# A fused attention and MLP block on one core: modulation, z and the last columns of w3 in column tiles and plain products, gb inside w4, a new order

## The chip, the cores and the metric

The kernel runs on one core of a Trainium2 chip. The metric is device time in microseconds (us) of one execution, the median of several runs. Five engines run their own instruction streams in order: PE multiplies matrices (PEld loads its stationary operands), DVE, ACT and POOL do elementwise work, SP issues nearly all transfers.

## The reference

S = 2048 rows, D = 512, H = 32 heads of 16, F = 1376, all in float32:

```
mod = silu(c) @ w_mod                      # 1 x 3072 = sa, ca, ga, sb, cb, gb
h   = layernorm(x) * (1 + ca) + sa
q, k, v = split(h @ wqkv)                  # 32 heads of 16
phi(t)  = concat(softmax(t @ w_phi), softmax(-(t @ w_phi)))   # 32 features a head
kv  = sum over rows of phi(k)^T v ;  z = sum over rows of phi(k)
o   = (phi(q) kv) / (phi(q) z + 1e-6)
x   = x + ga * (o @ wo)
g   = layernorm(x) * (1 + cb) + sb
s   = gelu(layernorm(g) @ w1), its four quarters shifted by +1, -1, +2, -2 rows
y   = g + s @ w2
out = x + gb * (y + gelu(layernorm(y) @ w3) @ w4)
```

## The kernel before

Rows go in eight chunks of 256, each of two tiles of 128. The attention needs kv and z over all rows before any output row, so the program has three stages: keys, values and queries of all chunks (until about 150 us), the attention's output with wo and then w1, w2 chunk by chunk (to about 370 us, beside the first half of the MLP), and the rest of the MLP (w3, gelu, w4). Most large products are made exact with fp32r halves: an operand is split into a high part and a remainder (`hi_lo`), and three products replace one (`three`). w3 and w4 are multiplied block-wise with seven products instead of eight, from sums of weight blocks and of activation blocks; the last 96 columns of w3 don't fill such a block and are treated apart (`up_last`, `load_last`, `load_w4_last`).

Names: `xl` is a tile of x, `xn` its normalized form, `pt` a transpose in PSUM (L481), `hh` the modulated and transposed chunk, `pp` general products in PSUM, `rk` raw rows of the q and k weights, which PE folds with w_phi (`bd` is w_phi as a block-diagonal matrix; one fold is 4 products of 128x128), `w` finished weights, `ke` and `qe` the features, `kva` the sum for kv, `za` the running sum of features from which z comes, `oT` the attention's output, `n` and `nT` the normalized rows of the second stage, `sh` the shifted rows, `gg` and `gl` high parts and remainders of gelu, `ac` the four accumulators of the w4 product, `uu` small temporaries, `xb` and `xc` the rows of the sum at the end. `const` is any small constant, `ones` among them.

Modulation: sa and ca are needed as columns (`mod_cols`, L532 on): the four 512 KB pieces of w_mod land as `mod2`; ca comes from products with one moving column, sa from a DVE sum and four more such products with `ones`. The other four are needed as rows that stand on all partitions (`mod_rows`, L549): 16 pieces of 256 KB are scaled by silu(c) and summed on ACT, DVE and POOL (`mod_acc`), and a product of `ones` with the sum puts the result on all partitions. z (L835) is `ones` times `za`, and eight copies take each head's piece out of it.

The order of all instructions is written out: `ORDER` is a table of operation numbers, each with a letter where it says which of DVE, ACT and POOL does it, `SLOT` one of buffer numbers. `plan.op` registers an operation with its reads and writes; `emit` issues all in the table's order, and each engine runs its share in that order. The operation's cost in `plan.op` only served to make the table. Each warm operation at the start (L501) is four products of `ones` with itself, whose result nobody reads. SP has at most eight transfers in flight.

```
def mms(items, w, r, ...):                       # products on PE; L472 issues them
def act(o, i, f, scale, bias, alts) / ts / tt / stt   # ACT; DVE or POOL where the table says so
def load(o, src, nbytes) / store(dst, i, nbytes)      # SP
```

Of the kernel before, what the change touches and what calls it, by code (L numbers as in the profile page):

```python
# [367 lines left out]
def body(ctx: ExitStack, tc, x, wqk_t, wv_d, wo_d, w1_d, w2_d, w3_d, w4_d, c_d, wmod_d, id_d, cst_d, cst2_d, out):  # L368
# [1024 lines left out]
```

## Time and profile before

| | us |
|---|---|
| median of 3 runs | 570.16 (569.96 to 570.29) |
| profiled execution | 570.87 |
| its span, first to last instruction | 569.1 |
| PE busy | 558.2 (98%) |
| DVE busy | 494.0 (87%) |
| POOL busy | 361.8 (64%) |
| ACT busy | 350.5 (62%) |
| mean granted clock of PE | 0.995 |

1.8 us of the profiled execution lie outside its span. In the rows of a timeline, the first number is when a group starts, the second how long it takes; "x" is the number of instruction records, and a product in plain float32 makes two records (two passes). What stands in square brackets is the idle time of the engine just before, and what ended it.

### The profile page before, as it was taken

Reading aid. Unit: us, or ns where it says so; the run is one execution under the profiler, and the core shown is the slowest. Engines: PE = TensorE matmul, PEld = TensorE weight load, DVE = VectorE, ACT = ScalarE, POOL = GpSimd, SP = SyncE. Lnnn points to the kernel's source line nnn. Section 1 sums busy time; section 2 is a strip of 40 time slices with the busy share of each in tenths; the row PEclk is TensorE's granted clock in tenths of the full one; section 3 lists DMA queues with packets and bytes.
Section 4 is the critical chain, followed back from the end, with each engine's and each line's share of the span. In section 5 each row is a group of like instructions: output and inputs, shape, how many; then the busy total and the mean of one; then the engine's idle time right before and its main releaser. Section 6 shows DMA issues by size and latency. Waiting matters only on the chain.

```text
span 569.1 us, 12257 instructions
## 1 busy us (share of the span) xinstructions
PE 558.2 (98%) x4460; PEld 502.4 (88%) x4460; DVE 494.0 (87%) x910; ACT 350.5 (62%) x826; POOL 361.8 (64%) x372
## 2 busy tenths in 40 slices
PE   9999999999999889999999999999999999999996
PEld 9998888788787678888879898999999999999995
DVE  3699999989899999999998777879777969898886
ACT  5699997733514767888787865865643544255530
POOL 3268978889699998998974744545444433113423
PEclk9899999999999999999999999999999999999999
DMA  8985430342646755778787896995976485828322
GB/s 327 341 270 185 168 131 29 121 131 75 222 163 238 246 157 153 288 245 313 241 263 239 299 322 226 341 357 192 390 264 219 174 285 159 324 88 272 112 75 74
DMA packets 56908, 124.06 MB, mean 218 GB/s; under 512 B 6864, under 2 KB 18384, under 8 KB 52752
## 3 DMA queue, kind: packets, MB, share of 16 engines
q1 hardware_dynamic: 56560, 123.21, 63.1%
q8 instruction: 35, 0.57, 0.4%
q14 instruction: 25, 0.20, 0.1%
q10 hardware_dynamic: 288, 0.07, 0.1%
HBM read 88.92 MB, written 34.34 MB: 217 GB/s over the span
## 4 chain that ended last, share of the span: by engine, by line
PE 83%; DVE 7%; POOL 4%; DMA 3%; ACT 1%; issue 1%; SPq 0%; DVEq 0%; POOLq 0%
PE pp L472 36%; PE pa L472 24%; PE ac L472 19%; PE pt L481 2%; DMA dram<-yt 2%; PE kva L472 1%; DVE q L443 1%; DVE pz L443 1%; POOL ez L421 1%; DMA dram<-qe 1%; POOL qe L421 1%; DMA dram<-h 1%; POOL e L421 1%; ACT n L402 1%; DVE oT L419 1%
## 5 line engine op out<-in xcount | busy, mean ns | idle before, releaser
L472 PE MATMUL pa<-bH,wq 128*128 128x256 f32 x840 | 106.8, 281 | 0.0
L472 PE MATMUL ac<-w,gg 128*128 128x256 f32 x840 | 106.0, 282 | 0.0
L472 PEld LDWEIGHTS pa<-bH,wq 128*128 128x128 f32 x840 | 103.0, 189 | 0.9 <-issue 0.2
L472 PEld LDWEIGHTS ac<-w,gg 128*128 128x128 f32 x840 | 101.8, 189 | 1.7 <-issue 1.7
L472 PE MATMUL pp<-w,hh 128*128 128x512 f32 x384 | 92.4, 396 | 0.0
L472 PEld LDWEIGHTS pp<-w,hh 128*128 128x128 f32 x384 | 71.0, 188 | 15.9
L472 PE MATMUL pp<-w,sh 128*128 128x512 f32 x192 | 49.0, 398 | 0.4 <-POOL sh L991 0.4
L472 PE MATMUL pp<-w,oT 128*128 128x512 f32 x192 | 47.6, 398 | 0.8 <-ACT oT L402 0.7
L472 PE MATMUL pp<-hh,w 128*128 128x256 f32 x384 | 48.1, 283 | 0.0
L472 PEld LDWEIGHTS pp<-hh,w 128*128 128x128 f32 x384 | 46.4, 188 | 1.9 <-issue 1.3
L472 PEld LDWEIGHTS pa<-nT,w 128*128 128x128 f32 x384 | 46.0, 188 | 1.8 <-DVE nT L419 1.0
L472 PE MATMUL pa<-nT,w 128*128 128x256 f32 x384 | 47.3, 280 | 0.1
L472 PEld LDWEIGHTS pp<-w,oT 128*128 128x128 f32 x192 | 35.4, 188 | 9.9 <-ACT oT L402 1.2
L472 PEld LDWEIGHTS pp<-w,sh 128*128 128x128 f32 x192 | 34.7, 188 | 9.3 <-issue 0.8
L582 POOL TENSOR_TENSOR rs<-mv,const 128x2 f32<-128x2 f32 x31 | 22.9, 740 | 28.3 <-ACT mv L589 28.1
L421 POOL TENSOR_TENSOR gg<-cu,gg 128x128 fp32r<-128x128 f32 (+1 forms) x25 | 17.2, 692 | 36.5 <-PE ac L472 26.7
L421 POOL TENSOR_TENSOR ez<-e,const 128x1024 f32<-128x1024 f32 x14 | 34.0, 2433 | 4.6 <-ACT const L402 4.4
L402 ACT ACTIVATE cu<-pa 128x512 f32<-128x512 f32 (+1 forms) x45 | 22.7, 516 | 19.1 <-PE pa L472 11.1
L402 ACT ACTIVATE gg<-cu 128x256 fp32r<-128x256 f32 (+1 forms) x60 | 20.2, 357 | 21.7 <-PE ac L472 11.3
L402 ACT ACTIVATE qe<-qe 128x512 f32<-128x512 f32 x32 | 19.1, 625 | 20.1 <-POOL qe L421 12.4
L419 DVE TENSOR_TENSOR gg<-sg,gg 128x512 fp32r<-128x512 f32 x37 | 26.8, 730 | 3.6 <-PE ac L472 2.5
L402 ACT ACTIVATE gg<-sg 128x512 fp32r<-128x512 f32 x37 | 22.8, 622 | 11.4 <-DVE sg L419 3.6
(215 smaller groups left out, 1299.4 us busy)
## 6 DMA issues: line engine op xcount, KB each, us to landing
wq<-dram SPq DMA_DIRECT2D x32, 1024.0 KB, 5.8
dram<-ws SPq DMA_DIRECT2D x35, 256.0 KB, 3.2
xl<-in_x SPq DMA_DIRECT2D x32, 256.0 KB, 3.7
dram<-qe SPq DMA_DIRECT2D x16, 512.0 KB, 2.9
e<-dram SPq DMA_DIRECT2D x16, 512.0 KB, 4.2
raw<-in_w SPq DMA_DIRECT2D x18, 256.0 KB, 3.8
mod<-in_wmod SPq DMA_DIRECT2D x16, 256.0 KB, 4.5
dram<-xl SPq DMA_DIRECT2D x16, 256.0 KB, 3.4
```

The source lines that it names most:

```text
L402: nc.scalar.activation(o(), i(), func, **kw)
L419: dve = ("DVE", 71 + 1.04 * o.n + 90 * (isps(a) and isps(b)), lambda: nc.vector.tensor_tensor(o(), a(), b(), op=op))
L421: pool = ("Pool", cost, lambda: nc.gpsimd.tensor_tensor(o(), a(), b(), op=op))
L443: plan.op("DVE", 65 + 1.04 * a.n + 110 * isps(o), lambda: nc.vector.tensor_reduce(o(), a(), axis=AX.X, op=op), [o], [a])
L472: nc.tensor.matmul(o(), a(), b(), start=s, stop=e, **kw)
L481: nc.tensor.transpose(o(), i(), ident())
L582: plan.op("Pool", 540 + 10 * m, lambda: nc.gpsimd.tensor_tensor(r(), v(), mhalf[:, :m](), op=OP.pow), [r], [v, mhalf])
```

## The change

Five parts and a new table.

1. **Columns.** silu(c) is copied onto 32 columns (`wide`). For each of the four `mod2` pieces, four products with 32 stationary columns and 256 moving ones stand beside each other in the four column tiles of the array, one for each half of sa and ca. ACT copies the sum, PE transposes it twice, and two DVE operations write the columns.
2. **Rows.** All four rows come from 16 products of `wide` with the 16 pieces (32 stationary, 512 moving columns, one row a column tile), accumulated in one bank. 1 is added to cb's part, four 2 KB stores put the rows into DRAM, and each row is later loaded back onto all partitions (`mod_row`). The scaling and summing on ACT, DVE and POOL goes.
3. **z.** Tiles 14 and 15 are no longer added to `za`; z is made of three parts (`za` and the two tiles) by four column-tiled products of 256 moving columns each, and one copy.
4. **The last 96 columns of w3.** `up_last` uses 96 stationary columns; in the w4 product, three products with 96 rows for each of the two tiles take the place of four with 128 and two with 64 rows.
5. **gb inside w4.** Each of the 11 pieces of w4 is multiplied by gb after it lands (four of these on DVE, seven on POOL), before the block sums are made. y * gb + x is made before the w4 product's end, so that a chunk ends with one addition and the store.
6. `ORDER` and `SLOT` are new throughout.

```diff
 ORDER = (
...
 )
...
 BIAS = {"start": 1, "late": 2, "ln_act": [1, 2, 3, 4, 5, 6, 7], "pair": [0, 1, 2, 3, 4, 5, 6, 7], "qpool": [0, 2, 4,
-        6, 8, 9, 10, 11, 12, 13, 14, 15], "tw": "any"}
+        6, 8, 9, 10, 11, 12, 13, 14, 15], "tw": "any", "zpe": [14, 15]}
...
@@ -509,49 +507,43 @@
...
-    cols = T("const", [P, 2, NK])
...
-    def mod_acc(j):
-        acc = T("acc")
-        for k in range(NK):
...
-                act(acc, raw, scale=sv[:, 0:1], alts=("DVE", "Pool"))
...
-                act(raw, raw, scale=sv[:, k:k + 1], alts=("DVE", "Pool"))
-                tt(acc, acc, raw, OP.add, "any")
-        return acc
+    cols, wide = T("const", [P, 2, NK]), T("const", [P, NK, 32])
 
     def mod_cols():
 
-        acc, p = T("acc"), T("pp", [P, 2, NK])
+        act(wide, sv[:, :, None].bc([P, NK, 32]), alts=("DVE",))
+        p, r, pc = T("pp", [P, HD]), T("mod", [P, HD]), T("pp", [P, 2, P])
         for k in range(NK):
             raw = T("mod2", [P, 2, D])
             load(raw, wmod_d[k * P:(k + 1) * P, :2 * D].rearrange("p (j n) -> p j n", j=2), 2 * P * D * 4)
-            if k == 0:
-                act(acc, raw[:, 0, :], scale=sv[:, 0:1], alts=("DVE",))
-            else:
-                stt(acc, raw[:, 0, :], sv[:, k:k + 1], acc, OP.mult, OP.add)
-            mms([(p[:, 1, b:b + 1], raw[:, 1, b * P:(b + 1) * P], sv[:, k:k + 1], k == 0 and b == 0, False)
-                 for b in range(NK)], [p], [raw, sv], skip=True)
-        mms([(p[:, 0, b:b + 1], acc[:, b * P:(b + 1) * P], ones[:, 0:1], False, b == NK - 1) for b in range(NK)],
-            [p], [acc, ones], skip=True)
+            mms([(p[32 * (2 * j + h):32 * (2 * j + h + 1)], wide[:, k, :], raw[:, j, h * HD:(h + 1) * HD], k == 0, k == NK - 1)
+                 for j in range(2) for h in range(2)], [p], [wide, raw], skip=True, tiles=4)
+        act(r, p, alts=("DVE",))
+        transp([(pc[:, i, :], r[:, i * P:(i + 1) * P]) for i in range(2)], [pc], [r])
         for j in range(2):
-            ts(cols[:, j, :], p[:, j, :], float(j), None, OP.add, None)
-
-    def mod_rows(j, plus, tag="const"):
-        acc = mod_acc(j)
-        p = T("pp")
-        mms([(p, ones, acc, True, True)], [p], [ones, acc])
+            ts(cols[:, j, :].re("p (h i) -> p h i", (2, 2), h=2).perm("p h i -> p i h", (1, 0)), pc[:, :, 64 * j:64 * (j + 1):32], float(j), None, OP.add, None)
+
+    mods = T("dram", [NK, D])
+
+    def mod_rows():
+
+        p, r = T("pp"), T("mod")
+        for k in range(NK):
+            raw = [T("mod") for _ in range(NK)]
+            for j in range(NK):
+                load(raw[j], wmod_d[k * P:(k + 1) * P, (2 + j) * D:(3 + j) * D], P * D * 4)
+            mms([(p[32 * j:32 * (j + 1)], wide[:, k, :], raw[j], k == 0, k == NK - 1) for j in range(NK)], [p], [wide, *raw],
+                skip=True, tiles=4)
+        act(r, p, alts=("DVE",))
+        ts(r[64:96], p[64:96], 1.0, None, OP.add, None)
+        for j in range(NK):
+            plan.op("SP", 475, lambda j=j: nc.sync.dma_start(mods()[j:j + 1, :], r()[32 * j:32 * j + 1, :]), [mods[:, :]], [r],
+                    lat=D * 4 / 380., land=1500 + D * 4 / 300.)
+
+    def mod_row(j, tag="const"):
         r = T(tag)
-        ts(r, p, plus, None, OP.add, None)
+        plan.op("SP", 475, lambda: nc.sync.dma_start(r(), mods()[j - 2:j - 1, :].to_broadcast([P, D])), [r], [mods],
+                lat=P * D * 4 / 380., land=2200 + P * D * 4 / 225.)
         return r
 
...
@@ -785,7 +777,7 @@
               tt_ == 0 and g < 4, tt_ == NT - 1 and g > 2 * NG - 5) for g in range(2 * NG)],
             [kva], [vv, e], skip=True, tiles=4)
         first.append(e)
-        if tt_:
+        if tt_ and tt_ not in BIAS["zpe"]:
             tt(zacc, first[0] if tt_ == 1 else zacc, e, OP.add, "any")
 
     hh0 = h_chunk(0)
@@ -809,10 +801,10 @@
             kv_add(ks[t], vs[t], c * TPC + t)
         plan.at(f"w{c}")
         if c == 1:
-            ga = mod_rows(2, 0.0, "acc")
-            cb1 = mod_rows(4, 1.0)
+            mod_rows()
+            ga = mod_row(2, "acc")
         if c == 2:
-            sb = mod_rows(3, 0.0)
+            cb1, sb = mod_row(4), mod_row(3)
...
-    zbc = T("const", [P, NG, 2 * DH])
-    for j in range(2):
-        p = T("pp", [P, NG // 2, HG, 2 * DH])
-        mms([(p.re("p g a f -> p (g a f)", (D,)), ones, zacc[:, j * D:(j + 1) * D], True, True)], [p],
-            [ones, zacc[:, j * D:(j + 1) * D]])
-        for a in range(HG):
-            act(zbc[32 * a:32 * (a + 1), NG // 2 * j:NG // 2 * (j + 1), :], p[32 * a:32 * (a + 1), :, a, :])
+    zbc, p = T("const", [P, NG, 2 * DH]), T("pp", [P, NG, 2 * DH])
+    parts = [zacc] + [e for t, e in enumerate(first) if t in BIAS["zpe"]]
+    for n, e in enumerate(parts):
+        mms([(p[32 * a:32 * (a + 1)], ones[:, :32], e.re("p (g a f) -> p g a f", (NG, HG, 2 * DH), a=HG, f=2 * DH)[:, :, a], n == 0,
+              n == len(parts) - 1) for a in range(HG)], [p], [ones, e], skip=True, tiles=4)
+    act(zbc, p)
...
     def load_last():
...
+        t = T("w", [P, 2 * NK * n9 + 2 * D], FR)
+        hi, lo = last["w3"] = [t[:, i * NK * n9:(i + 1) * NK * n9].re("p (k n) -> p k n", (NK, n9), k=NK) for i in range(2)]
+        last["w4"] = [t[:, 2 * NK * n9 + i * D:2 * NK * n9 + (i + 1) * D] for i in range(2)]
...
     def load_w4_last():
         plan.at("w42")
...
-        hi_lo(*last["w4"], raw, lo_eng="any", alts=("DVE", "Pool"))
...
+        raw, n = T("raw")[:n9], n9
+        load(raw, w4_d[2 * NP * P:, :], n * D * 4)
+        tt(raw, raw, gb[:n], OP.mult, "any")
+        hi_lo(last["w4"][0][:n], last["w4"][1][:n], raw, lo_eng="any", alts=("DVE", "Pool"))
...
@@ -1070,6 +1055,7 @@
             load(raw[i].re("p a n -> p (a n)", (D,)), w4_d[k * P:(k + 1) * P, :], P * D * 4, marks[after] if after else None)
+            tt(raw[i], raw[i], gb.re("p (a n) -> p a n", (2, HD), a=2), OP.mult, "any")
...
     plan.at("gb")
-    gb = mod_rows(5, 0.0, "gb")
+    gb = mod_row(5, "gb")
...
@@ -1190,15 +1176,11 @@
         items = []
         for k in range(NK):
             x = xs[k // 2]
-            items += three(p, last["w3"][0][:, k, :], last["w3"][1][:, k, :], x[:, 0, k % 2, :], x[:, 1, k % 2, :],
+            items += three(p[:n9], last["w3"][0][:, k, :], last["w3"][1][:, k, :], x[:, 0, k % 2, :], x[:, 1, k % 2, :],
                            k == 0, k == NK - 1)
         marks["up"] = mms(items, [p], [*last["w3"], *xs], after=marks.get("up"))
-        act(p, p, AF.Gelu_apprx_tanh)
-        act(g[:, 0, :], p)
-        for t in range(2):
-            sl = slice(t * P, (t + 1) * P)
-            tt(g[HF * t:HF * (t + 1), 1, sl], p[:HF, sl], g[:HF, 0, sl].f32(), OP.subtract)
-        tt(g[n9:, 0, :], p[n9:], g[n9:, 0, :].f32(), OP.subtract)
+        act(p[:n9], p[:n9], AF.Gelu_apprx_tanh)
+        hi_lo(g[:n9, 0, :], g[:n9, 1, :], p[:n9])
         cells[s, h, "last"] = g
...
@@ -1282,12 +1264,10 @@
             gs = ready(s, h, j)
             if j == NP - 1:
                 g = cells[s, h, "last"]
-                ps = [acc[2 + t].re("p a n -> p (a n)", (D,)) for t in range(2)]
-                sl = [slice(t * P, (t + 1) * P) for t in range(2)]
-                items = [(ps[t], g[:, 0, sl[t]], w, False, False) for t in range(2) for w in last["w4"]]
-                for t, w in enumerate((last["w4"][0], last["w4h"])):
-                    items.append((ps[t], g[HF * t:HF * (t + 1), 1, sl[t]], w[HF * t:HF * (t + 1)], False, False))
-                mms(items, acc[2:], [g, *last["w4"], last["w4h"]], skip=True, both=232)
+                for t in range(2):
+                    sl = slice(t * P, (t + 1) * P)
+                    mms(three(acc[2 + t].re("p a n -> p (a n)", (D,)), g[:n9, 0, sl], g[:n9, 1, sl], last["w4"][0][:n9],
+                              last["w4"][1][:n9], False, False), [acc[2 + t]], [g, *last["w4"]], skip=True)
...
@@ -1303,8 +1283,11 @@
         xs = []
         for t in range(TQ):
             plan.at(f"out{c * TQ + t}")
-            x1 = T("xb")
+            x1, x2 = T("xb"), T("xc")
             load(x1, x1_s[c * TQ + t], P * D * 4)
+            load(x2, x2_s[c * TQ + t], P * D * 4)
+            tt(x1, x1, gb, OP.mult, "either")
+            tt(x1, x1, x2, OP.add, "either")
             xs.append(x1.re("p (a n) -> p a n", (2, HD), a=2))
...
         for t, x1 in enumerate(xs):
-            tt_ = c * TQ + t
-            p = acc[2 + t]
+            rows_, p = slice((c * TQ + t) * P, (c * TQ + t + 1) * P), acc[2 + t]
             if c < NC - 1:
                 tt(x1, x1, p, OP.add)
-            plan.at(f"out{tt_}")
-            x1, x2 = x1.re("p a n -> p (a n)", (D,)), T("xc")
-            load(x2, x2_s[tt_], P * D * 4)
-            tt(x1, x1, gb, OP.mult, "either")
-            tt(x1, x1, x2, OP.add, "either")
-            if c < NC - 1:
-                store(out[tt_ * P:(tt_ + 1) * P, :], x1, P * D * 4)
+                store(out[rows_, :], x1.re("p a n -> p (a n)", (D,)), P * D * 4)
                 continue
-            p = p.re("p a n -> p (a n)", (D,))
             for a in range(2):
-                sl = slice(a * HD, (a + 1) * HD)
-                v = T("uu", [P, HD])
-                tt(v, p[:, sl], gb[:, sl], OP.mult)
-                tt(x1[:, sl], x1[:, sl], v, OP.add, "either")
-                store(out[tt_ * P:(tt_ + 1) * P, sl], x1[:, sl], P * HD * 4)
+                tt(x1[:, a, :], x1[:, a, :], p[:, a, :], OP.add)
+                store(out[rows_, a * HD:(a + 1) * HD], x1[:, a, :], P * HD * 4)
```

PE's start, around the columns, in the kernel before (`mod_18` and the like are the `mod2` pieces, `const_173` silu(c), `const_67` is `ones`, `const_161` the identity):

```order
L472 MATMUL pp_178<-bd_133,rk_107 128x128 x4
L472 MATMUL pp_188<-const_67 128x128 x4
L472 MATMUL pp_197<-const_67 128x128 x4
L472 MATMUL pp_210<-const_173,mod_18_109 128x1 x4
L472 MATMUL pp_210<-const_173,mod_19_111 128x1 x4
L472 MATMUL pp_210<-const_173,mod_10_89 128x1 x4
L472 MATMUL pp_210<-const_173,mod_20_113 128x1 x4
L472 MATMUL pp_210<-const_67,acc_206 128x1 x4
L472 MATMUL pp_257<-bd_133,rk_124 128x128 x4
L481 MATMUL pt_273<-const_161,xn_248 128x128
```

The same place in the changed kernel (`const_220` is `wide`, `const_110` the identity, `mod_284` the copied sum):

```order
L470 MATMUL pp_181<-bd_85,rk_69 128x128 x4
L470 MATMUL pp_195<-const_67 128x128 x4
L470 MATMUL pp_209<-const_67 128x128 x4
L470 MATMUL pp_215<-const_67 128x128 x4
L470 MATMUL pp_231<-const_67 128x128 x4
L479 MATMUL pt_244<-const_110,xn_241 128x128
...
L470 MATMUL pp_250<-mod_21_118,const_220 32x256 x4
L470 MATMUL pp_250<-mod_24_129,const_220 32x256 x4
L470 MATMUL pp_250<-mod_20_115,const_220 32x256 x4
L470 MATMUL pp_250<-mod_19_112,const_220 32x256 x4
```

Ahead of the columns stood seven warm operations, a fold and two more warm ones; now four warm operations, three folds, a warm one, a fold, four more warm ones and four transposes do. Between the columns and the first projection (`pp<-w,hh`) stood seven folds and twelve transposes; now four folds, twelve transposes and the two of the columns' sum do.

SP's stream, where the 16 w_mod pieces for the rows end in the changed kernel. They are rows 22 to 40 of the stream now; in the kernel before they were spread over rows 15 to 62:

```order
L447 DMA mod_414<-in_wmod 128x512
L447 DMA mod_452<-in_wmod 128x512
L447 DMA const_459<-in_cst 128x32
L447 DMA mod_464<-in_wmod 128x512
L447 DMA mod_502<-in_wmod 128x512
L447 DMA wr_505<-in_w 128x4x256
L447 DMA xl_518<-in_x 128x512
```

The products that read them (`pp_513`) stand on PE behind two k projections, two projections on the other operand side (`pp<-hh,w`, 24 products each) and eight transposes. The buffer of the last piece is one that held raw v weights before.

PE's end, in the kernel before (two accumulators, `ac_7568` and `ac_7549`):

```order
L472 MATMUL ac_7568<-w_2950,gl_7379 128x512 x2
L472 MATMUL ac_7549<-w_2950,gl_7379 128x512 x2
L472 MATMUL ac_7568<-w_2950,gl_7379 128x512
L472 MATMUL ac_7549<-w_4721,gl_7379 128x512
L472 MATMUL ac_7549<-w_4699,gg_7434 128x256
L472 MATMUL ac_7549<-w_4721,gg_7434 128x256
L472 MATMUL ac_7549<-w_4699,gg_7471 128x256
L472 MATMUL ac_7568<-w_4699,gg_7434 128x256
```

and in the changed one:

```order
L470 MATMUL ac_7477<-w_4723,gg_7460 128x256
L470 MATMUL ac_7472<-w_4512,gg_7302 128x256
L470 MATMUL ac_7472<-w_4636,gg_7302 128x256
L470 MATMUL ac_7472<-w_4512,gg_7338 128x256
L470 MATMUL ac_7472<-w_4646,gg_7397 128x256 x2
L470 MATMUL ac_7472<-w_4646,gg_7469 128x256
L470 MATMUL ac_7472<-w_3401,gl_7399 128x512 x3
L470 MATMUL ac_7472<-w_4723,gg_7356 128x256
```

Before, the two accumulators end nearly together; now `ac_7477` is complete twelve products ahead of `ac_7472`.

More of the change, by code (lines that the diff above doesn't have):

```diff
@@ L178 @@
-    "xn": "531f9ae64275bkai",
-    "acc": "faaf09",
-    "mod2": "1203",
-    "kva": "5",
-    "za": "1",
-    "hh": "2839cde8",
-    "pt": "54320106046160741015674650715354",
-    "raw": "k0hibd367de683l1l2e067jfi81fd",
-    "k1": "0153254515324021",
-    "ke": "4523970423790524",
-    "k2": "3011024041255323",
-    "vv": "8lh6d3b5ib2bbd2h",
-    "qe": "9701537660847318",
-    "q1": "3204341052034512",
-    "qt": "3g2hbdhfbj3f",
-    "mod": "lh37ed4gi2bj1i4e",
-    "kvs": "3",
-    "pz": "2",
@@ L225 @@
-    "uu": "g2gh4delkc92",
-    "xc": "fh716ihlfaj08jgi",
+    "pp": "220713137460513130726250130736452156623250562150350242655640233106337040236475364074236205244305"
+          "0264523076314576566475",
+    "bd": "21",
+    "w": "015647ac312085acd1472e",
+    "rk": "4305gjfc",
+    "xl": "69bh787540k8hfeld8l94dgi5kgefa9e15h3haj6h0g1g0k1",
+    "st": "14d03afdijc9e748d3jfa56a82dd5gicj",
+    "mv": "75g37c0f342fijc9e74g42f4f83h1h508",
+    "rs": "8ah6b64e718g352fiachc8gbd67ij31fd",
+    "nm": "cbei295289j1gh0a5b6dh0a1b6gh051ejb19e069b9i0372cea7246b9",
@@ new lines @@
+    "xn": "li57adhc62e1g7hf",
+    "mod": "2g02l3d6gc4ahbjif9",
+    "mod2": "2310",
+    "kva": "7",
+    "za": "3",
+    "hh": "2839bde8",
+    "pt": "62734534406134412605764776744175",
+    "raw": "ie6j3db918067i5ba3bd8b2i374k",
+    "k1": "1023412053032235",
+    "ke": "5401972654096758",
+    "k2": "4135124524302403",
+    "vv": "8kj12c23a3a427h3",
+    "qe": "7632124183485930",
+    "q1": "3205154112045012",
+    "qt": "251f2cf142if",
+    "acc": "g",
+    "kvs": "e",
+    "pz": "1",
+    "q2": "01542120",
@@ new lines @@
+    "e": "2019671475317268",
+    "ez": "9344109306823539",
+    "q3": "2342031053453415",
+    "q5": "13354132",
+    "pT": "8204364682195019",
+    "oT": "56d84596",
+    "nT": "b5edee49",
+    "n": "c3i27b7hbhci4je9",
+    "h": "6e03c42670g1f5ak",
+    "gf": "82513315",
+    "sh": "9674d74b",
+    "pa": "265074073020125713247706145423176025304315767174272605356272",
+    "wr": "88204",
+    "ws": "ai0ll7dkjc49e0h89721c8i9d9lg23k31db",
+    "gb": "l",
+    "tw": "85951",
+    "bL": "70832848",
@@ new lines @@
+    "nb": "iaj5ichae92b6a5j",
+    "yt": "c15hk4j6h0g12d4b",
+    "bH": "26413769526413251056073179124136",
+    "tr": "dc46c4ak6a697chb",
+    "wq": "9b6739e6b3096b309360b9630b3069b3069b",
+    "cu": "6cde9hbf57i24150ec3b482bge36a1c5df7a026k",
+    "gl": "ikgh7446",
+    "ac": "27366417652036057134430137645120",
+    "gg": "41097410967908794761830495637428916045287091536120305630927402598712693247051986",
+    "sg": "2i4i407gajdh7a8f7ia9icj09h59aii9be6igb19",
+    "xb": "836923dkf1j8h5kc",
+    "xc": "j28jbkjfc00k4e3d",
@@ L227 @@
+    "uu": "kikf29jg",
 }
@@ L457, in store, with mms @@
                 lat=nbytes / 380., land=1500 + nbytes / 300.)
-    def mms(items, w, r, skip=False, hold=(), after=None, duty=1.0, tiles=1, both=0):
-        cost, rec = 150 * (tiles > 1) - both, 0
+    def mms(items, w, r, skip=False, hold=(), after=None, duty=1.0, tiles=1):
+        cost, rec = 150 * (tiles > 1), 0
         for o, a, b, *_ in items:
@@ L957, in phase_a @@
         return sh, hs
-    NP, NB, n9, HF = FT // 2, 7, F - FT // 2 * 2 * P, P // 2
+    NP, NB, n9 = FT // 2, 7, F - FT // 2 * 2 * P
     w3s = T("dram", [P, NB * NP, 4 * P])
@@ L1028, in load_last @@
         plan.at("w3l")
-        t = T("w", [P, 4 * D], FR)
-        hi, lo = last["w3"] = [t[:, i * D:(i + 1) * D].re("p (k n) -> p k n", (NK, P), k=NK) for i in range(2)]
-        last["w4"] = [t[:, (2 + i) * D:(3 + i) * D] for i in range(2)]
-        raw = T("raw", [P, NK, P])
-        load(raw[:, :, :n9], w3_d[:, 2 * NP * P:].rearrange("(k p) n -> p k n", p=P), D * n9 * 4)
-        load(raw[:, :, n9:], w3_d[:, F - (P - n9):].rearrange("(k p) n -> p k n", p=P), D * (P - n9) * 4)
+        t = T("w", [P, 2 * NK * n9 + 2 * D], FR)
+        hi, lo = last["w3"] = [t[:, i * NK * n9:(i + 1) * NK * n9].re("p (k n) -> p k n", (NK, n9), k=NK) for i in range(2)]
+        last["w4"] = [t[:, 2 * NK * n9 + i * D:2 * NK * n9 + (i + 1) * D] for i in range(2)]
+        raw = T("raw", [P, NK, n9])
+        load(raw, w3_d[:, 2 * NP * P:].rearrange("(k p) n -> p k n", p=P), D * n9 * 4)
         hi_lo(hi, lo, raw, lo_eng="any", alts=("DVE", "Pool"))
@@ L1038, in load_w4_last @@
         plan.at("w42")
-        raw, n = T("raw"), F - (P - n9)
-        load(raw[:n9], w4_d[2 * NP * P:, :], n9 * D * 4)
-        load(raw[n9:], w4_d[n:, :], (P - n9) * D * 4)
-        hi_lo(*last["w4"], raw, lo_eng="any", alts=("DVE", "Pool"))
-        raw = T("raw")[HF:]
-        load(raw, w4_d[2 * NP * P:2 * NP * P + HF, :], HF * D * 4)
-        position(2 * NB * NP + 1)
-        last["w4h"] = store8[-1][:, 6:8, :].re("p a n -> p (a n)", (D,))
-        act(last["w4h"][HF:], raw, alts=("DVE", "Pool"))
+        raw, n = T("raw")[:n9], n9
+        load(raw, w4_d[2 * NP * P:, :], n * D * 4)
+        tt(raw, raw, gb[:n], OP.mult, "any")
+        hi_lo(last["w4"][0][:n], last["w4"][1][:n], raw, lo_eng="any", alts=("DVE", "Pool"))
     store8 = []
```

48 lines of the change are left out of this document (removed), and 248 rows, old and new, of the table ORDER.

## The prediction

> **What bounds the kernel now.** First the engines' busy time and the chain of work that ended last, then busy time by stretches.
>
> ```profile
> span 569.1 us, 12257 instructions
> PE 558.2 (98%) x4460; PEld 502.4 (88%) x4460; DVE 494.0 (87%) x910; ACT 350.5 (62%) x826; POOL 361.8 (64%) x372
> PE 83%; DVE 7%; POOL 4%; DMA 3%; ACT 1%; issue 1%; SPq 0%; DVEq 0%; POOLq 0%
> ```
>
> ```profile
> 0.00:10.00 10.00, 9.03 (x55) 9.03 (x56) 2.50 (x10) 4.75 (x12) 4.10 (x13) 1.00 0.82 298
> 10.00:20.00 10.00, 10.00 (x80) 10.00 (x80) 3.87 (x9) 6.26 (x14) 2.37 (x5) 0.86 1.02 375
> 200.00:250.00 50.00, 48.01 (x372) 40.46 (x371) 49.29 (x80) 40.03 (x92) 46.85 (x42) 1.00 0.62 209
> 300.00:350.00 50.00, 49.56 (x341) 45.06 (x340) 38.27 (x71) 36.06 (x99) 24.47 (x34) 1.00 0.81 283
> ```
>
> The columns of a window are its length, then busy us of PE, PEld, DVE, ACT and POOL, PE's granted clock, the transfers' share and GB/s. PE has work nearly always and carries 83% of the chain, so work that PE no longer has, or does earlier, is time won, as long as the others keep up. DVE is as full in the middle (49.29 of 50): there a gain of PE counts only if DVE loses work too. In the first 20 us PE is busy and DVE is not, and much of what PE does there is warm products that nobody reads. So the start has to be read group by group.
>
> ```profile
> 0.97 9.36 PE L472 MATMUL pp<-const 128*128 128x128 f32 x56 [0.97 <-POOL const L499]
> 12.85 3.63 PE L472 MATMUL pp<-const,mod 128*128 128x1 f32 x32
> 17.27 2.06 PE L472 MATMUL pp<-bd,rk 128*128 128x128 f32 x8
> 19.12 1.77 PE L481 MATMUL pt<-const,xn 128*128 128x128 f32 x8
> 20.73 1.95 PE L472 MATMUL pp<-bd,rk 128*128 128x128 f32 x16
> 22.51 0.60 PE L481 MATMUL pt<-const,xn 128*128 128x128 f32 x4
> 22.95 3.74 PE L472 MATMUL pp<-bd,rk 128*128 128x128 f32 x32
> 26.44 3.04 PE L472 MATMUL pp<-w,hh 128*128 128x512 f32 x12
> 29.32 1.47 PE L481 MATMUL pt<-const,xn 128*128 128x128 f32 x12
> 33.46 8.66 PE L472 MATMUL pp<-hh,w 128*128 128x256 f32 x72
> 41.96 2.97 PE L472 MATMUL pp<-w,hh 128*128 128x512 f32 x12
> ```
>
> Each row is a group: start, duration, records. One group follows right behind the other, so the difference of two starts is a group's price: the first projection's 12 products take 29.32 - 26.44 = 2.88, .24 each, and 72 of 256 moving columns 8.50, .118 each. The first projection starts at 26.44. 32 fold records take 3.49, .109 each; the 8 behind the N=1 products (one moving column) take 1.85, .23 each, and the 8 transposes then 1.61, .20 each, where four took .44. The granted clock of that window is 0.86: the N=1 products are followed by a stretch at half rate that costs 8 x .12 + 8 x .09 = 1.7 us. The first warm records are slow too: 56 in 9.36, which is about 30 at .21 and 26 at .109.
>
> **The change part by part.** *Start.* After has on PE, in this order: 32 warm records, three folds (24), a warm group (8), a fold (8), four warm groups (32), four transposes, the columns' 16 products, four transposes, two of the columns' sum, a fold, eight transposes, three folds, then the first projection. Priced by the rows above: .97 + 30 x .21 + 2 x .109 = 7.5; the next 40 records 4.4, at 11.9; four warm groups 3.5, at 15.4; four transposes .4, at 15.8. By then the columns' w_mod pieces have to be there. They and all that goes ahead of them are about 4.3 MB; at 298 GB/s up to 10 us and 375 from there they have landed by 13.5. Two normalized tiles have to be there too:
>
> ```profile
> 9.34 0.70 POOL L582 TENSOR_TENSOR rs<-mv,const 128x2 f32<-128x2 f32 x1
> 11.94 0.80 ACT L402 ACTIVATE xn<-xl,nm,rs 128x512 f32<-128x512 f32 x1
> ```
>
> x was loaded first and its scale was done at 10.04; now the weights of four folds go ahead of it, 1 MB or 2.8 us at 375 GB/s, so the scale comes at 12.9 and two normalized tiles with a small operation of .3 ahead at 14.8. Both are in time. A column tile's product is one of four that stand beside each other; the nearest row is of tiles of 64*32:
>
> ```profile
> 201.26 1.11 PE L472 MATMUL pp<-pT,const 64*32 64x256 f32 x32
> L402 ACT ACTIVATE uu<-ac 128x256 f32<-128x256 f32 x7 | 2.7, 386 | 10.5 <-PE ac L472 10.2 <-DVE xb L419 0.2
> L402 ACT ACTIVATE pt<-pt,const 128x256 f32<-128x256 f32 x20 | 10.4, 529 | 2.4 <-PE pt L481 1.5 <-DVE pt L411 0.6
> L402 ACT ACTIVATE hh<-pt 128x512 fp32r<-128x512 f32 x13 | 7.6, 594 | 0.4
> L419 DVE TENSOR_TENSOR hh<-pt,hh 128x512 fp32r<-128x512 f32 x16 | 10.7, 680 | 0.7 <-ACT hh L402 0.7
> ```
>
> 32 records of 256 columns take 1.11 us there, .035 each, where one alone takes .225 (a pass of 512 takes .45, below). So tiles do run beside each other, and I price a set of four products, two passes each, at 2 x .225 = .45: 1.8 for the columns, end at 17.6. The copy (.39) lies beside four transposes (.44); two transposes (.22) and two small DVE operations bring the columns at 18.8. PE goes on meanwhile: a fold, eight transposes and three folds, .87 + .88 + 2.6, end at 22.6. The chunk's scale, copy and remainder behind its last transpose (.53, .59, .68) end at 22.2. So the first projection starts at 23.0 (.4 for handing over) instead of 26.44, with four more transposes (.44) already done. **Gain 3.9.** If a stretch at half rate comes here too (1.7), 2.2; with nothing handed over late, 4.3.
>
> *Rows.*
>
> ```profile
> L472 PE MATMUL pp<-acc,const 128*128 128x512 f32 x8 | 4.2, 605 | 0.0
> L421 POOL TENSOR_TENSOR acc<-acc,mod 128x512 f32<-128x512 f32 x8 | 10.3, 1298 | 1.3 <-DVE acc L419 1.0
> L402 ACT ACTIVATE mod<-mod,const 128x512 f32<-128x512 f32 x10 | 7.0, 712 | 0.0
> L419 DVE TENSOR_TENSOR acc<-acc,mod 128x512 f32<-128x512 f32 x4 | 3.0, 753 | 0.1
> L438 DVE SCALAR_TENSOR_TENSOR acc<-mod,const,acc 128x512 f32<-128x512 f32 x3 | 2.3, 752 | 0.1
> L419 DVE TENSOR_TENSOR za<-za,ke 128x1024 f32<-128x1024 f32 x4 | 5.1, 1276 | 0.5 <-POOL ke L421 0.5
> ```
>
> On PE eight records, 3.6 without their overlap (.45 a pass); after, four sets of two such passes, 3.6: zero. ACT and POOL lose 7.0 and 10.3; DVE loses 3.0, the columns' 2.3 and, as the table gives it one `za` sum where it had four, 3.8: 9 us before 150 us. POOL later gets seven products of w4 with gb, 1.3 each; its 24.47 of 50 in 300 to 350 us, ahead of the first w4 product, hides them, so I count nothing; without that cover, the 9 us at POOL's 4% of the chain show .4. The stores and broadcast loads of rows: ga is needed first, for wo, whose products run around 180 us, over 100 us behind its load; nothing. The row stores stand on SP ahead of raw v weights, which are needed at about 53 us and land at about 46 by the stream's order; nothing.
>
> *z.*
>
> ```profile
> 150.04 1.88 PE L472 MATMUL pp<-za,const 128*128 128x512 f32 x4
> 151.84 0.65 PE L472 MATMUL kva<-ke,vv 128*32 128x64 f32 x32
> ```
>
> 1.80 before; three sets of two passes of .225 after, 1.35. **Gain .45.** z also no longer waits for two sums and eight copies; PE does not wait there now.
>
> *Last 96 columns.*
>
> ```profile
> 380.32 1.50 PE L472 MATMUL ac<-w,gl 128*128 128x512 f32 x6
> 381.75 1.45 PE L472 MATMUL ac<-w,gg 128*128 128x256 f32 x10
> ```
>
> 1.43 for four full products and a pair of half rows. Twelve full products of 512 columns in the chain of work:
>
> ```profile
> 72.47 2.78 PE pp L472 x12
> ```
>
> Six at that pace (.232) take 1.39, at the .24 above 1.44. Times eight, a gain of .3 to a loss of .1; I take **.2**.
>
> The Trainium skill ("TensorEngine Tiling (Array Packing)", Tiling Modes, Key Properties) says that changing the tiling mode drains TensorE. That fits the half-row pair: beside four products at .232 it leaves .50, where the pair itself is .24. By that rule the column tiles' three new stretches would cost about .27 each, and the sum would be .8 us less of a gain.
>
> *Tail.*
>
> ```profile
> 562.55 1.34 PE L472 MATMUL ac<-w,gg 128*128 128x256 f32 x9
> 565.00 0.76 DVE L419 TENSOR_TENSOR xb<-xb,uu 128x256 f32<-128x256 f32 x2
> ```
>
> PE ends at 563.89, DVE's last addition at 565.76, 1.87 later. After, one tile is added before PE ends, and two additions (.76) with .2 to start them remain. **Gain .9**; the store and the 3.3 us to the span's end stay.
>
> *Order of the middle.* PE's largest waits:
>
> ```profile
> 197.41 1.09 PE L481 MATMUL pt<-const,n 128*128 128x128 f32 x8 [1.47 <-ACT n L402]
> 213.50 0.63 PE L481 MATMUL pt<-const,n 128*128 128x128 f32 x4 [1.89 <-DVE oT L419]
> ```
>
> Counted product by product at the prices above, the new order puts about 12 us between a tile's wo products and the transposes of its normalized rows, where some 14 to 17 passed. If those chains stay as long, the waits grow by 2 to 4; DVE's 9 us less, and its earlier z, may shorten them or end them (3.4 less). I take **0**.
>
> **Sum**: 3.9 + .45 + .2 + .9 = 5.45. The profiled execution took 570.87, so 565.4; the median stands .7 below it: **564.7**. With the start between 2.2 and 4.3, the last columns between their ends and the middle 2 either way, this case goes from 562 to 568.5.
>
> **Rivals.** *DVE doesn't let the head start through* (49.29 of 50): the 3.9 is gone by 250 us, and z, the last columns and the tail stay, 568.6. Against it: DVE loses 9 us ahead of that stretch. *The waits of the middle grow* by 2 to 4, 566.7 to 568.7. For it, DVE and POOL are fullest there (49.29 and 46.85 of 50) and fewer products lie between; against it, the same 9 us. *Slower: the row products hold PE.* PE runs in order, and its 16 row products stand where it should arrive at 35.3 (23.0 + 24 x .24 + 48 x .118 + 8 x .11). The last w_mod piece is issued once DVE has used the raw v weights in its buffer; with the other transfers at the pace of the rows above that is about 32, and it lands at 36 at the earliest. If DVE or SP is late, PE stands idle with all the second chunk's projections queued behind; from a landing after 41 on the whole gain is gone, and a landing at 43 makes 572.4 (7.7 of idle time). For it: 16 pieces now have to land for one set of products, where one row had four; against it: nothing in the transfers' 298 to 375 GB/s delays them by that much. *The column tiles do not run beside each other*: each set costs four times, 3 x (1.8 + 3.6 + 1.35) = 20 more, 585; the .035 a record speaks against it.
>
> The Trainium skill ("TensorE: Matmul & The Clock Gate", Part 1) says that the clock is halved after an activity window that found TensorE idle. The .86 behind the N=1 products agrees. By it the changed start, which has none, keeps its full rate.
>
> **How the numbers follow.** Forecast .58; DVE rival .16; waits of the middle .15; row products .08; no overlap .03. 0.2%, 1.1 us, is about what a measurement can tell here. Faster by more: the forecast and most of the DVE and middle cases, .81; slower the last two, .11; same .08. The range is 559.5 to 569.5: below it the middle's waits would have to go and the start's best end come; above lie the last two rivals and little of the others.
>
> **What would show it.** The first projection at 23.0 and the granted clock near 1 in 10 to 20 us; the row products without a wait, at about 35; 1.35 for z; six products of the last columns in 1.39 to 1.44; .96 from PE's end to DVE's last addition; the middle's waits still at 3 to 4 us. A lead at 250 us that is under 2 us of the start's, or PE waiting for `mod`, shows the prediction wrong in the way of that rival.

## The result, and the profile after

The changed kernel takes 560.96 us (560.28 to 561.27, 4 runs) beside 570.22 for the kernel before: a ratio of 0.9832, 95% interval 0.9815 to 0.9849. That is 9.3 us less where 5.5 were forecast; it lies within the stated range, near its lower end.

The busy times and the chain of work of the profiled execution (561.05 us):

```profile
span 559.3 us, 12228 instructions
PE 550.7 (98%) x4498; PEld 499.6 (89%) x4498; DVE 482.0 (86%) x892; ACT 338.5 (61%) x798; POOL 353.8 (63%) x367
PE 92%; POOL 3%; DVE 2%; DMA 2%; ACT 1%; issue 0%; DVEq 0%; POOLq 0%
```

The span fell by 9.8 us, PE's busy time by 7.5. PE now carries 92% of the chain instead of 83%: what went is not only work of PE but also the pieces of the chain that lay on DVE and on transfers. PE's start, in the timeline after:

```profile
16.68 0.66 PE L479 MATMUL pt<-const,xn 128*128 128x128 f32 x4 [0.95 <-DVE xn L409]
17.26 1.93 PE L470 MATMUL pp<-mod,const 128*32 128x256 f32 x32
19.13 0.66 PE L479 MATMUL pt<-const,xn 128*128 128x128 f32 x4
24.34 5.84 PE L470 MATMUL pp<-w,hh 128*128 128x512 f32 x24
36.67 3.64 PE L470 MATMUL pp<-mod,const 128*32 128x512 f32 x32
40.24 3.04 PE L470 MATMUL pp<-w,hh 128*128 128x512 f32 x12
```

The first projection starts at 24.34 (23.0 forecast, 26.44 before), after a wait for the normalized tiles. The columns' 32 records cost 1.87, the rows' 3.57, close to the 1.8 and 3.6 of the forecast: column tiles do run beside each other. The two windows in which it was to be seen:

```profile
0.00:10.00 10.00, 8.73 (x55) 8.57 (x56) 1.21 (x4) 1.49 (x2) 3.02 (x11) 1.00 0.80 235
10.00:20.00 10.00, 9.05 (x95) 7.62 (x94) 7.38 (x20) 6.79 (x18) 2.65 (x5) 1.00 1.04 401
```

The granted clock is 1.00 in the second one, 0.86 before: there is no half-rate stretch any more. The transfers, though, moved 235 GB/s in the first 10 us, where 298 went before.

PE's waits behind the first 10 us, the view of waits, first before and then after:

```profile
PE pt L481 <- DVE oT L419: 1.9, 1, 1.9
PE pt L481 <- ACT n L402: 1.5, 1, 1.5
PE pp L472 <- ACT oT L402: 0.7, 1, 0.7
PE pp L472 <- POOL sh L991: 0.4, 1, 0.4
```

```profile
PE pp L470 <- DVE pT L750: 1.4, 1, 1.4
PE pt L479 <- DVE xn L409: 0.9, 1, 0.9
PE pa L470 <- DVE nT L417: 0.6, 1, 0.6
PE pt L479 <- ACT n L400: 0.2, 1, 0.2
```

Of the waits in the middle, 4.5 us became 2.2 (all but the one for `xn`, which is of the start). z, and the sums for kv, in the timeline after:

```profile
146.04 0.64 PE L470 MATMUL pp<-za,const 128*32 128x256 f32 x8
146.49 1.05 PE L470 MATMUL pp<-ke,const 128*32 128x256 f32 x16
147.36 0.63 PE L470 MATMUL kva<-ke,vv 128*32 128x64 f32 x32
159.25 1.99 PE L470 MATMUL kva<-ke,vv 128*32 128x64 f32 x128
161.17 3.09 PE L470 MATMUL pp<-hh,w 128*128 128x256 f32 x24
```

z takes 147.36 - 146.04 = 1.32 where it took 1.80. And the end:

```profile
554.62 0.52 PE L470 MATMUL ac<-w,gg 128*128 128x256 f32 x3
555.18 0.75 DVE L417 TENSOR_TENSOR xb<-xb,ac 128x256 f32<-128x256 f32 x2 [0.44 <-PE ac L470]
```

PE ends at 555.14, DVE's last addition at 555.93: 0.79 after it, where it was 1.87.

By place, of the 9.8 us of span: the start 2.5 (2.1 earlier and four transposes more), z 0.5, the last 96 columns 1.1 (measured below), the end 1.1, the middle's waits 2.3. A sixth item was not in the forecast. The 512 records of the kv sums stood in 12 stretches before and stand in 6 now; a stretch of 32 costs 0.59 before (151.84 to 152.43 by the rows of z there), so four of them 2.36, and one of 128 costs 1.92. Six stretches fewer are worth about 0.9. Together 8.4; 1.4 us are spread over small gaps that I did not assign.

### The profile page after: what moved, and what is told of

Its sections match the earlier page's. It is cut to its first block, busy times and chain, and to the rows that moved or that the text cites. A ratio compares the mean times of both kernels' runs of the same rounds, so it can differ in the third digit from the quotient of the medians.

```text
span 559.3 us, 12228 instructions
## 1 busy us (share of the span) xinstructions
PE 550.7 (98%) x4498; PEld 499.6 (89%) x4498; DVE 482.0 (86%) x892; ACT 338.5 (61%) x798; POOL 353.8 (63%) x367
## 4 chain that ended last, share of the span: by engine, by line
PE 92%; POOL 3%; DVE 2%; DMA 2%; ACT 1%; issue 0%; DVEq 0%; POOLq 0%
PE pp L470 41%; PE pa L470 27%; PE ac L470 20%; PE pt L479 3%; PE kva L470 1%; DMA xl<-in_x 1%; POOL ez L419 1%; POOL e L419 1%; ACT xn L400 1%; DMA const<-in_c 1%; POOL rs L574 1%; POOL qe L419 0%; DVE pp L436 0%; DVE h L436 0%; DVE q L441 0%
## 5 line engine op out<-in xcount | busy, mean ns | idle before, releaser
L470 PEld LDWEIGHTS ac<-w,gg 128*128 128x128 f32 x840 | 103.1, 188 | 0.8
L419 POOL TENSOR_TENSOR gg<-cu,gg 128x128 fp32r<-128x128 f32 (+1 forms) x28 | 19.9, 714 | 27.5 <-PE ac L470 7.7
L400 ACT ACTIVATE cu<-pa 128x512 f32<-128x512 f32 (+1 forms) x39 | 20.1, 530 | 27.6 <-PE pa L470 24.4
L419 POOL TENSOR_TENSOR e<-e,q 128x1024 f32<-128x1024 f32 x16 | 31.7, 2000 | 1.9 <-DVE q L417 1.9
L419 POOL TENSOR_TENSOR za<-za,ke 128x1024 f32<-128x1024 f32 x12 | 28.8, 2400 | 3.2 <-DVE ke L417 2.7
L419 POOL TENSOR_TENSOR ez<-e,const 128x1024 f32<-128x1024 f32 x12 | 29.8, 2490 | 0.3 <-PE pp L470 0.2
```

The costliest lines, as they stand in the source:

```text
L400: nc.scalar.activation(o(), i(), func, **kw)
L419: pool = ("Pool", cost, lambda: nc.gpsimd.tensor_tensor(o(), a(), b(), op=op))
L470: nc.tensor.matmul(o(), a(), b(), start=s, stop=e, **kw)
```

## The experiments

Each is compared with runs of the kernel before on the same chip; ratios are to those, with their 95% interval.

### What the last 96 columns are worth

The kernel before, with the half-row pair as full products of the high parts (the remainder's part of this product is left out):

```diff
-                for t, w in enumerate((last["w4"][0], last["w4h"])):
-                    items.append((ps[t], g[HF * t:HF * (t + 1), 1, sl[t]], w[HF * t:HF * (t + 1)], False, False))
+                for t in range(2):
+                    items.append((ps[t], g[:, 0, sl[t]], last["w4"][0], False, False))
```

> The kernel before, with the pair of half-row products for the remainder of the last 96 columns replaced by two full 128-row products of the high parts (so the remainder's part of that product is left out; six full products a chunk as in the change). By my sum's row (1.43 us for the step, 1.39 to 1.44 after) the gain is 0.2 us, at most 0.3. By the trace after, the pair costs 0.62 us a chunk with the ways there and back (0.42 for itself, 0.09 ahead of it, 0.10 in the second gap behind it), where two full products take 0.464: a gain of 8 x 0.155 = 1.2 us.

569.47 us beside 570.64, a ratio of 0.9980 (0.9968 to 0.9991): 1.1 us, interval 0.5 to 1.8. My 0.2 is outside it, 1.2 inside. Where the rest was hidden can be read from the group behind the pair. In the kernel before the last one, nine `gg` products at 562.55, stands in the prediction with 1.34; in the timeline of this run, without the pair, the same group takes 1.22:

```profile
561.97 1.22 PE L472 MATMUL ac<-w,gg 128*128 128x256 f32 x9
```

In each of the eight chunks the group behind is 0.10 to 0.16 shorter, 0.9 in all; the steps themselves are 0.5 shorter in all. I had priced the step up to the start of the next group, and so missed the larger part.

### Does the load of the rows' sums make the middle's waits?

The kernel before, without them (each row is then its first quarter alone):

```diff
                 act(raw, raw, scale=sv[:, k:k + 1], alts=("DVE", "Pool"))
                 tt(acc, acc, raw, OP.add, "any")
+                for o in plan.ops[-2:]:
+                    o.fn = lambda: None
...
```

> The kernel before without 12 scalings and 12 additions of the rows' sums on ACT, DVE and POOL (each row is then its first quarter alone); all transfers and PE's products stay. If the load of these engines makes PE's waits in the middle (4.1 us at 189, 197 and 213 us), it gains 2 to 3 us. If the waits come from where the table puts the products and z's chain, less than 0.5 us.

570.52 us, a ratio of 1.0002 (0.9990 to 1.0013): nothing. PE's waits in this run, the view of waits:

```profile
PE pt L481 <- DVE oT L419: 1.9, 1, 1.9
PE pt L481 <- ACT n L402: 1.4, 1, 1.4
PE pp L472 <- ACT oT L402: 0.7, 1, 0.7
```

They are those of the kernel before, to 0.1 us. In the old table, the load theory falls. The other side of it: idle work on the three engines in the changed kernel.

```diff
+    scr = [T("const", [P, HD]) for _ in range(3)]
...
+    for i in range(60):
+        plan.extra[200 + 6 * i + 3 * (i % 2)] = (sca, dve, gps)[i % 3]
...
-        for o in self.order():
+        for n, o in enumerate(self.order()):
             o.fn()
+            if n in self.extra:
+                self.extra[n]()
```

> The changed kernel with 20 idle products of 128x256 on each of DVE, POOL and ACT (8.4, 13.6 and 7.2 us in all) between some 30 and 130 us, where the rows' sums stood. By the load theory the waits in the middle come back, 2 to 3 us; by the theory that the places in the table made them, less than 0.5 us; if DVE were the bound all along, 8 us.

575.54 us, a ratio of 1.0091 (1.0074 to 1.0108), some 15 us slower than the changed kernel, more than any of the theories said. PE now waits between 60 and 200 us for features, in the view of waits for that stretch:

```profile
PE pp L473 <- POOL ke L422: 4.1, 2, 2.8
PE pp L473 <- DVE ke L420: 2.2, 1, 2.2
```

So in the first stage of the new table POOL and DVE have little room. The middle did not change: PE is 13.2 us late ahead of it (its products with `kvs`, the finished sum for kv, start at 177.38, in the changed kernel at 164.20) and 13.2 at the first large group of `pa` products, those of the normalized rows `nT` (210.81 and 197.66), and its waits there are the changed kernel's. Nor is all of the loss waiting: the granted clock was 0.91 from 80 to 100 us and 0.94 from 160 to 180, where the changed kernel has 1.00. The load was larger than planned, 21.1 us on DVE and 14.2 on POOL instead of 8.4 and 13.6. And it was larger than the relief, which two windows show, up to 150 us, before and after:

```profile
0.00:150.00 150.00, 149.03 (x1190) 129.32 (x1191) 130.96 (x191) 105.23 (x231) 112.08 (x96) 0.99 0.54 182
```

```profile
0.00:150.00 150.00, 147.78 (x1247) 125.46 (x1248) 128.71 (x189) 94.91 (x215) 105.55 (x93) 1.00 0.58 195
```

DVE was relieved of 2.3 us there and POOL of 6.5, not of the 9 and 10 that the sums had cost: the table gave them other work. A smaller load, 10 idle products on POOL and 6 on DVE in the same way:

> The changed kernel with 10 idle products of 128x256 on POOL and 6 on DVE (6.2 and 2.5 us) between some 40 and 130 us: as much as POOL (112.1 to 105.5 us) and DVE (131.0 to 128.7 us) were relieved of up to 150 us. If the relief was needed for the new table, 2 to 6 us slower than the changed kernel; if these engines have room for it there, under 1 us.

561.98 us, a ratio of 0.9855 (0.9840 to 0.9870) where the changed kernel has 0.9825 to 0.9832: about 1.5 us slower, likely rather than certain, as the intervals overlap or touch; that is less than the 2 to 6 of one theory and more than the 1 of the other. The products took 7.6 us on POOL and 6.0 on DVE, so DVE got back more than its relief. The view of waits of this run:

```profile
PE pp L473 <- DVE pT L761: 1.4, 1, 1.4
PE pa L473 <- DVE nT L420: 0.6, 1, 0.6
PE pp L473 <- POOL ke L422: 0.4, 1, 0.4
```

The middle's waits, for `pT` and `nT`, are those of the changed kernel; what is new is a wait for features. The `kvs` products start 1.03 later than in the changed kernel (165.23 and 164.20), the large group of `pa` products 1.04 later (198.70 and 197.66), and the span is 1.0 longer. So the relief is worth something in the first stage of the new table and nothing in the old one, and it does not make the shorter waits of the middle.

### Does z's chain make them?

In the changed kernel, z's four operations behind one more v projection in the table (`664 665 666 667` moved behind `565`):

> The changed kernel with z's products and copy one v projection (12 products of 512 columns, 2.9 us) later on PE and ACT. If z's earlier chain is what emptied the middle of waits, the time grows by 2 to 3 us, with DVE standing at the first ez. If DVE and POOL have slack there, by less than 0.5 us.

565.19 us, a ratio of 0.9910 (0.9897 to 0.9923): 4 to 5 us slower, more than expected. z itself came 4.1 us later (150.13 instead of 146.04), as PE also waited for the v rows of a kv sum ahead of it. The views of waits of DVE and of PE say where it went:

```profile
DVE ez L428 <- ACT const L411: 3.9, 1, 3.9
```

```profile
PE pp L481 <- DVE pT L761: 3.1, 1, 3.1
PE pp L481 <- DVE const L428: 0.8, 1, 0.8
```

DVE stands 3.9 us for z, ahead of `ez`, the features times z, and PE pays it some 35 us on, at the features' transposes: 0.8 that the changed kernel does not wait, and 3.1 where it waits 1.4. These 2.5 us are the 2 to 3 expected. Two more things are in the total: the wait for the v rows, 0.8, and what stands behind the wait of 3.1, in PE's timeline:

```profile
186.38 4.63 PE L481 MATMUL pp<-hh,w 128*128 128x256 f32 x24
```

Up to the next group, at 190.85, these 24 records take 4.47, where the changed kernel's take 2.94 (182.99 to 185.93); the granted clock from 180 to 190 us is 0.83 instead of 1.00. That is another 1.5; about 1 us of the three is won back elsewhere. In the new table, then, a later z makes the middle wait. So the kernel before was given the change's z, its sums for tiles 14 and 15 dropped from `za`, and moved one v projection ahead (`678 679` moved from behind `826` to behind `577`):

```diff
+    parts = [zacc, first[14], first[15]]
+    def z_products():
+        for n, e in enumerate(parts):
+            for a in range(HG):
+                nc.tensor.matmul(zp[32 * a:32 * (a + 1)](), ones[:, :32](), ...)
...
+            if tt_ > 13:
+                plan.ops[-1].fn = lambda: None
```

> The kernel before with the change's z alone: tiles 14 and 15 are not added to za (4.9 us less on POOL at 144 us), three sets of column-tiled products and one copy take the place of two full products and eight copies, and z stands one v projection (2.9 us) earlier on PE. If z's chain makes the middle's waits, 2 to 4 us faster, with POOL's 4.4 us of idle time ahead of its first ez and most of PE's waits at 189 to 213 us gone. If the middle's gain came from the rest of the new table, only z's own 0.45 us.

571.39 us, a ratio of 1.0020 (1.0009 to 1.0030): a little slower. PE's largest waits are the old ones:

```profile
PE pt L486 <- DVE oT L424: 1.9, 1, 1.9
PE pt L486 <- ACT n L407: 1.5, 1, 1.5
```

z alone does not empty the old middle either. POOL, in its order, only stood longer ahead of its first ez (8.8 us, where it had been 4.4), now for a kv sum of PE that had kept its place. So of the two engines that make ez only DVE could use the earlier z; the old table with POOL free to use it too was not tried. With z early and without the rows' sums:

> The same, and without the 12 scalings and 12 additions of the rows' sums (left out, each row is its first quarter). If the sums' load matters once z no longer holds the middle, this is 1 to 2 us faster than with z alone; if not, the same within 0.5 us.

570.51 us, a ratio of 1.0012 (1.0000 to 1.0024). Neither, nor both: in the old table each engine's work behind z stands where it stood, and what was freed ahead of it became idle time.

### One instruction of the old middle

DVE's rows ahead of PE's largest wait, and POOL's row beside the first of them, in the timeline of the kernel before:

```profile
209.97 2.59 DVE L419 TENSOR_TENSOR ws<-wr,ws 128x256 fp32r<-128x256 f32 x1
212.68 0.68 DVE L419 TENSOR_TENSOR oT<-pp,oT 128x512 fp32r<-128x512 f32 x1
```

```profile
209.90 2.38 POOL L421 TENSOR_TENSOR ez<-e,const 128x1024 f32<-128x1024 f32 x1
```

A block sum that takes 0.41 elsewhere took as long as POOL's product beside it, and `oT`, for which PE stood 1.89, came behind. The sum was given to POOL (`1007` from its place to `1007G` behind `1004G`):

> The kernel before with one instruction moved: the sum of two w2 blocks (128x256, both operands and the result in SBUF) that took DVE 2.59 us at 209.97 instead of 0.41, beside POOL's ez of 2.38 us at 209.90, goes to POOL, right behind the block sum ahead of it. If PE's 1.89 us wait at 211.6 was this one collision, the wait goes and the time falls by 1 to 2 us. If DVE is simply full there (49.29 of 50), the wait moves to the next place and the time falls by less than 0.5 us.

570.28 us, a ratio of 0.9996 (0.9986 to 1.0006). The wait for `oT` is gone, and another stands for it. DVE and PE in the timeline of that run:

```profile
210.24 0.68 DVE L424 TENSOR_TENSOR oT<-pp,oT 128x512 fp32r<-128x512 f32 x1
212.62 2.53 DVE L424 TENSOR_TENSOR ws<-wr,ws 128x256 f32<-128x256 f32 x1
215.07 0.68 DVE L424 TENSOR_TENSOR nT<-pt,nT 128x512 fp32r<-128x512 f32 x1
```

```profile
215.89 0.35 PE L477 MATMUL pa<-nT,w 128*128 128x256 f32 x1 [1.05 <-DVE nT L424]
216.59 5.80 PE L477 MATMUL pa<-nT,w 128*128 128x256 f32 x47 [0.35 <-DVE nT L424]
```

The next block sum, 0.40 in the kernel before (at 215.06), now lasted 2.53 beside POOL's work, and PE's 1.89 became 1.40. This collision was moved by one block sum, and the stall moved with it.

### The start

The changed kernel with x loaded ahead of the folds' weights (SP's order `2 38 45 246 247 30 26 22 34 ...`), eight warm operations ahead of the folds and the ninth left out:

> The changed kernel with the four tiles of x loaded ahead of the four folds' weights, as in the kernel before, all warm operations but one ahead of the folds, and the last warm one left out. If the normalized tiles (PE stood 0.95 us for them at 15.7) and the column pieces' landing set the first projection, it starts 1.5 to 2 us earlier than 24.3 and the time falls by as much; if PE's own work in front of it sets it, by less than 0.5 us.

The changed kernel itself was repeated beside it on the same chip:

> The changed kernel unaltered, to stand beside the others on one chip: 9 us faster than before, as first measured.

With x first it is 559.08 us, 0.9805 (0.9791 to 0.9820); the changed kernel repeated, 560.14, 0.9825 (0.9809 to 0.9840). The intervals overlap, so the 1.1 us are likely rather than certain. The first projection starts 0.9 earlier. PE still stood before its transposes, in the timeline:

```profile
10.95 3.74 PE L476 MATMUL pp<-bd,rk 128*128 128x128 f32 x32
15.82 0.63 PE L485 MATMUL pt<-const,xn 128*128 128x128 f32 x4 [1.13 <-issue]
23.45 5.84 PE L476 MATMUL pp<-w,hh 128*128 128x512 f32 x24
```

The normalized tiles had long been there (their scales at 7). The transposes' PSUM buffer was that of a fold, which DVE had not read yet: I infer this from the order of buffers. Folds earlier and two warm operations left out:

> The changed kernel with the start of the kernel with x first, and on PE five warm operations, two folds, a warm one, two folds, the first transposes, a warm one, then the columns; two warm operations left out. With x first PE's transposes at 15.82 had waited for the fold's buffers, not for x, so the columns should end near 15.5 instead of 18.2 and the first projection start near 20.5 instead of 23.5: 2 to 3 us faster than with x first if PE stays the bound up to the middle; if the row pieces' landing (about 36) or DVE takes it back, under 1 us faster.

559.68 us, 0.9818 (0.9805 to 0.9832): no gain over the last, though the first projection started at 21.16. PE gave it back in the next chunk, and the timeline of ACT, then of PE, shows why:

```profile
25.13 0.60 ACT L405 ACTIVATE w<-pp 128x512 fp32r<-128x512 f32 x1 [2.98 <-PE pp L475]
```

```profile
32.17 0.66 PE L484 MATMUL pt<-const,xn 128*128 128x128 f32 x4 [1.42 <-POOL xn L414]
```

One fold had been put behind the first projection; ACT, in order, stood 2.98 us for it, and the second chunk's normalization stood behind. With that fold back ahead, and those transposes behind both query projections (`167` behind `135`):

> The kernel with the shorter start (columns ending near 15.8 us), with the last fold of the query weights back ahead of the first projection (ACT had stood 2.98 us for it, and the third and fourth tiles behind it), and the second chunk's first transposes behind both query projections. If the 1.42 us wait for those tiles is what gave the shorter start's gain back, the first projection starts near 21.6 and 1.5 us more are kept: about 558 us. If the lead is lost again at the next tight place, it stays at 559 to 560.

557.82 us, a ratio of 0.9764 (0.9744 to 0.9783): faster than both kernels, by 13 to 14 us and by 2 to 4 (2.3 to 3.1 by the times, which are of other chips, 3.5 to 3.9 by the ratios). The first projection at 21.88 and the rows at 34.21, with PE without a wait in between, in the timeline:

```profile
21.88 5.84 PE L475 MATMUL pp<-w,hh 128*128 128x512 f32 x24
27.55 5.85 PE L475 MATMUL pp<-hh,w 128*128 128x256 f32 x48
33.24 1.03 PE L484 MATMUL pt<-const,xn 128*128 128x128 f32 x8
34.21 3.64 PE L475 MATMUL pp<-mod,const 128*32 128x512 f32 x32
```

Of the 2.46 us that the rows' products start earlier than in the changed kernel, the time keeps about all.

## Why the prediction was right, and where it was not

**The bound.** PE set the end, as read: what it was spared or given earlier came out at the end where it did not wait for it further on, down to the last experiment. The half-rate stretch of the start went with the N=1 products: the granted clock from 10 to 20 us is 0.76 to 0.86 in all six profiled executions with them and 1.00 in all eight without. The Trainium skill ("TensorE: Matmul & The Clock Gate", Part 1) has the clock halved after a window that found TensorE idle. The slow stretch behind the 3.1 us wait with z late agrees; at the start the records show PE busy, so there it agrees only if N=1 products count as idle, which was not tried by itself.

**The start: 3.9 forecast, 2.5 measured.** The step that failed is the landing of transfers. "298 GB/s up to 10 us" was the rate of another order of loads; 235 went. So the scales of x came at 14.4 to 15.5 and not at 12.9, PE stood 0.95, and the columns ended at 19.13, not 17.6. With x first again, the start won back 0.9 of this.

**Rows and z: right.** 3.57 for 3.6 and 1.32 for 1.35. The rows' products started at 36.67 (35.3 forecast) and did not wait, so the slower rival did not come about; neither did the column tiles that do not overlap.

**The last columns: 0.2 forecast, 1.1 measured.** The mechanism was right and the term too small: the 0.10 to 0.16 in the group behind each pair were not counted. The rule of the Trainium skill that I had weighed beside this ("TensorEngine Tiling (Array Packing)", Tiling Modes, Key Properties), that a change of tiling mode drains TensorE, fits this pair, and the kv sums agree with it too, at 0.44 for three stretches fewer. For the new column tiles I had worked out 0.8 less of a gain by it, and the measured groups show that they hold the price without it.

**The end: 0.9 forecast, 1.1 measured**, by the path described.

**The middle: 0 forecast, 2.3 measured.** Here the step failed that counted the products between a wo product and its transposes, about 12 us where 14 to 17 had passed, and set a chain that stays as long against a relief that may end it, for 0. The chain did not stay as long: behind the first chunk's wo products, its transposes came after 13.8 us before (183.61 to 197.41, with a wait of 1.5) and after 11.1 now (180.38 to 191.46, without one). The case where waits grow did not occur. What the runs show: in the new table z must not come later (4 us later made 2.5 us of waits and a half-rate stretch), but work put back on POOL and DVE costs time only ahead of the middle and leaves its waits as they are; so the relief that I had weighed, DVE's above all, did not make the gain. In the old table neither the sums nor z changed the waits, alone or together, as far as z could be used there, and a single collision taken out came back at the next block sum. Which of the table's moves shortened the chain was not settled, and the cause of these 2.3 us stays open.

**DVE's relief.** "DVE loses 9 us ahead of that stretch" was the argument against the DVE rival. The conclusion held (the last experiment's lead of 2.46 us at the rows was 2.85 at the `pa` products around 262 us), but by the windows the relief was 2.3 us: the table had filled it again.

## What to carry to other kernels

When all engines run in a written order, work removed from an engine that is nearly full may be worth nothing, as here, until the order behind it is changed too; so price a removal and its new order together, test the removal alone before crediting it, and look in which stage a load that is put back costs its time. A long wait can cost more than itself: here 1.5 us of slow products stood behind one of 3.1. A change of the array's mode cost time in the group behind it as well: price a step up to where the pace is normal again. At a kernel's start, read which buffer a waiting instruction writes, not only which data it reads, and look what stands behind each instruction that waits, on its own engine.

## What the runs showed of the hardware

A DVE addition of 128x256 with both operands in SBUF took 2.59 us beside a POOL product of 2.38, and 0.41 elsewhere. The next one, with the first moved away, took 2.53 beside the last 0.3 us of a POOL product and two more POOL instructions, of 0.76 and 1.31. Both ended 0.3 us behind the last of these. The Trainium skill ("SBUF — State Buffer", Who interferes with whom) says that a DVE instruction with two SBUF inputs contends with a GpSimd instruction that reads SBUF, and that the ports they share are locked by one of them at a time; the trace agrees. The idle DVE products of the load, of the same size, took 0.41 to 2.15 us. That such a stall, moved, fell on the next instruction of its kind was new to me.

Transfers in the first 10 us reached 234 to 256 GB/s in five executions with the folds' weights first (the changed kernel twice, and three experiments on it) and 270 to 303 in nine with x first, three of them of the changed kernel with its loads reordered. So the rate at the start goes with the order of the loads; what it is in the order (the sizes of the pieces, or the queue's first descriptors) was not tried.
